# Seven block products for eight in the first product of a channel mix, on pairs of weight blocks in two passes

## The chip, the core and the metric

The kernel runs on one core of a Trainium2 chip. TensorE (PE) multiplies, VectorE (DVE) and ScalarE (ACT) work on tiles in SBUF and read PE's sums in PSUM, SyncE (SP) issues the DMAs. The metric is the device time of one execution in microseconds, as the median of three runs. Weights and inputs lie in DRAM at the start, the output is written back there.

## The reference

```python
B, H, S, D = 4, 8, 576, 64                     # tokens: 4 x 576 = 2304, columns C = 8 x 64 = 512
x = attention(q, k, v)                          # windowed and dilated heads, softmax
xk, xr = mixes of x and the token before it
v = relu(xk @ w_k) ** 2 @ w_v                   # 512 -> 1024 -> 512
x = sigmoid(xr @ w_r) * v
u = x + (relu(x^T @ w_tok1) @ w_tok2)^T         # token stage: 576 -> 256 -> 576
h2 = relu(u @ w_ch1) @ w_ch2                    # channel stage: 512 -> 1536 -> 512
out = u + h2
```

All arrays are fp32. w_ch1 is called w_c1 in the kernel, w_ch2 w_c2. The change concerns the channel stage, which computes `h2` and `out` for 2304 tokens.

## The kernel before

Stages follow one another: attention, the mix with `w_k`, `w_v` and `w_r`, the token stage, the channel stage. In the trace, the token stage's tiles begin at about 343 us and the channel stage has PE alone from about 409 us.

A matrix product in fp32 is made of parts. Each operand is split into a high half (fp32r, made by a copy) and a low half (what is left, made by a subtraction), and `mm3` (L441) issues three matmuls: high x high, high x low, low x high. A matmul has a stationary operand of 128 x 128 and a moving one of up to 512 columns. Thus one product with 512 rows in depth takes 4 x 3 matmuls for 128 rows of output.

Weights are read as pairs of 32-bit words. `weight` (L472) makes fp32 of them: a DMA into a raw tile, an ACT activation (Prelu), a DVE `tensor_scalar`, a DVE `scalar_tensor_tensor` on 16-bit halves; then the split, a copy (on ACT or DVE) and a subtraction (DVE).

The channel stage lies transposed: rows are columns of the model, columns are tokens. `u` (L822) is held in the slots `wv`, four batches of 576 tokens. It runs over chunks of 512 tokens, four full ones and a last one of 256 (L962 to L976). In each chunk:

- `prep_u` (L932) splits the four 128-row tiles of `u` into halves.
- `middle(c, m)` (L938), for 12 blocks m of 128 hidden columns, multiplies block m of `w_c1` with these four tiles into one of the PSUM banks 0 to 3, and then ACT takes the relu as the high half and DVE makes the low half.
- `result(c, m)` (L949) stands two blocks later in the program. It multiplies the 128 rows m of `w_c2` with that hidden block into banks 4 to 7, one for each 128 output rows, summed over all 12 blocks. After the last, DVE adds `u`, and a DMA on SP's queue stores the tile in `outT`.

All 24 blocks of channel weights are converted up to the end of the first chunk and stay in SBUF: four of `w_c1` ahead of the token stage in program order, the others as the first chunk comes to them (`weight_1`, `weight_2`).

The program is only recorded by that code. `Plan` keeps each operation with the operations that it depends on, and where an operation may run on ACT or DVE, both forms. `order()` (L287) is a list scheduler: it sums the costs of the PE operations in program order to due times, gives every other operation the due time that its readers need, and then, engine by engine, starts the ready operation that is due first, by a cost for each form and a delay for each pair of engines. What comes out is a fixed order for each engine's queue. `emit` issues everything from one line, so every row of the trace has that line (L399), and groups are told apart by tile names: `xt`, `x`, `wk`, `wr`, `wv`, `at`, `z`, `raw`, `unit` are slots of SBUF, `bank` is PSUM. Slots are used by several stages in turn: in the channel stage `wv` holds `u`, `xt` and `wk` hold `w_c1`, `x` (x2) and `at` hold `w_c2`, `z`, `y`, `wr` and part of `xt` hold split tokens and hidden blocks.

Of the kernel before, what the change touches and what calls it, by code (L numbers as in the profile page):

```python
# [61 lines left out]
    wk=[2048] * 4, wr=[1024] * 4, wv=[4 * S] * 4, z=[1536] * 6, y=[512],  # L62
# [85 lines left out]
class Plan:  # L148
# [35 lines left out]
    @staticmethod  # L184
    def _cells(a):
# [10 lines left out]
    def either(self, *options):  # L196
# [3 lines left out]
        local = [(k, a) for k, a in kw.items() if hasattr(a, "space") and "DRAM" not in str(a.space)]  # L200
# [212 lines left out]
def tile_model(nc, banks, units, cst, mu, w_k, w_v, w_r, w_t1, w_t2, w_c1, w_c2, outT):  # L413
# [27 lines left out]
    def mm3(out, lh, ll, rh, rl, first, last):  # L441

        nc.tensor.matmul(out=out, lhsT=lh, rhs=rh, start=first, stop=False)
        nc.tensor.matmul(out=out, lhsT=lh, rhs=rl, start=False, stop=False)
        nc.tensor.matmul(out=out, lhsT=ll, rhs=rh, start=False, stop=last)
# [31 lines left out]
    wv2 = [pair(("wv", m, 0), (2, C)) for m in range(4)]  # L477
# [9 lines left out]
    def weight(srcs, hi, lo, raw_ring, tmp_ring, zero=None):  # L487

        shape = tuple(hi.shape[1:])
        n = int(np.prod(shape))
# [12 lines left out]
        t = tmp_ring.tile(n)  # L510
# [7 lines left out]
        if len(shape) == 2:  # L518
            t = t.split(*shape)
        split(t, hi, lo)  # L520
# [21 lines left out]
    unit_r = ring(cut("wv", range(4), UQ + UK), ("z", 4, 0))  # L542
    v_r = ring(cut("wr", range(4), UV), ("z", 4, UQ + UK))
# [261 lines left out]
    for k in range(2):  # L805
# [6 lines left out]
    c1 = [  # L812
        tuple(at(xt512[2 * n + i], (4, 128), F32R) for i in range(2))
        for n in range(4)
    ]
    c1 += [pair(p, (4, 128)) for p in cut("wk", range(4), 1024)]
    c2 = [pair(p, (C,)) for p in cut("x2", (5, 6, 0, 1, 2, 3, 4), 1024)] + [pair(p, (C,)) for p in cut("at", (0,), 1024)]
    raw_c, tmp_c = ring([("wr", k, 0) for k in range(3)]), ring(cut("z", (5,), 512))
    hid_r = ring(z512[:8])
    x2h_r, x2l_r = ring(z512[9::2]), ring(z512[10::2])  # L820

    def u(b, kt, cs):  # L822
        return at(("wv", b, S * kt), (S,))[:, cs]

    def weight_1(m):
        if m < 4:
            for n in range(2):
                q = slice(2 * n, 2 * n + 2)
                weight([(everything, col_block(w_c1, m)[:, q, :])], c1[m][0][:, q, :], c1[m][1][:, q, :], raw_b, tmp_b)
        else:  # L830
            weight([(everything, col_block(w_c1, m))], *c1[m], raw_c, tmp_c)

    def weight_2(m):
        weight([(everything, words(w_c2)[rows(m), :])], *c2[m], raw_c, tmp_c)
# [5 lines left out]
    for m in range(4):  # L840
        weight_1(m)
# [25 lines left out]
    def turn(t):  # L867
# [36 lines left out]
    for t in range(13, 17):  # L904
# [150 lines left out]
```

## Time and profile before

| | before |
|---|---|
| median of three runs | 708.95 us (708.1 to 709.75) |
| profiled execution | 708.25 us, its span 706.5 us |
| busy share of the span | PE 98%, PEld 85%, DVE 54%, ACT 41%, POOL 0% |
| mean granted clock of TensorE | 0.999 |
| DMA | 56.20 MB, mean 80 GB/s |

PEld is the load of the stationary operand, which overlaps PE. The span lies within the profiled execution's time, the rest is around it. A share over the whole span mixes the stages: DVE is busy 9 tenths in the slices from about 340 to 410 us and 1 to 3 tenths after that. The chain that ended last tells through which engine the end of the program was reached, step by step backward.

### The profile page before, as it was taken

How to read it: one execution, taken by the hardware profiler on the slowest of the kernel's cores; microseconds unless marked ns; L12 is line 12 of the kernel's file. 1: busy time of each engine (PE TensorE's matmuls, PEld its weight loads, DVE VectorE, ACT ScalarE, POOL GpSimd, SP SyncE). 2: the span in 40 equal slices, each digit the busy share in tenths (PEclk: the TensorE clock that was granted, in tenths of full speed). 3: DMA queues.
4: the chain of work that ended last, by engine and by line, in shares of the span. 5: the costliest groups of instructions: out<-in, count | busy, mean ns of one | idle time of the engine just before them, and what ended most of it. 6: DMA issues, size and time to landing. Idle time of an engine off the chain costs nothing.

```text
span 706.5 us, 10519 instructions
## 1 busy us (share of the span) xinstructions
PE 692.7 (98%) x4081; PEld 599.5 (85%) x4081; DVE 382.0 (54%) x879; ACT 287.8 (41%) x818; POOL 2.1 (0%) x22
## 2 busy tenths in 40 slices
PE   7889999999999999999999999999999999999997
PEld 6678888988988888888889988888888888888897
DVE  5999995794694695774999941132123112311211
ACT  5989864582463463543778621121121111111110
POOL 0000000000000000000000000000000000000000
PEclk9999999999999999999999999999999999999999
DMA  8987333142221002013444500001001000100010
GB/s 321 389 315 275 115 95 95 49 148 84 89 79 31 16 9 66 17 31 100 133 148 150 150 0 1 1 0 60 0 1 60 0 1 0 60 1 0 8 53 31
DMA packets 27234, 56.20 MB, mean 80 GB/s; under 512 B 2480, under 2 KB 10032, under 8 KB 27184
## 3 DMA queue, kind: packets, MB, share of 16 engines
q1 hardware_dynamic: 27184, 55.53, 23.7%
q8 instruction: 32, 0.52, 0.3%
q14 instruction: 18, 0.15, 0.1%
HBM read 50.80 MB, written 4.72 MB: 79 GB/s over the span
## 4 chain that ended last, share of the span: by engine, by line
PE 88%; DMA 6%; ACT 3%; DVE 2%; issue 0%; SPq 0%; DVEq 0%; ACTq 0%
PE bank L399 88%; DMA x<-w_k 2%; ACT z L399 1%; DMA wr<-units 1%; DVE z L399 1%; ACT x L399 1%; DMA wv<-units 1%; DMA raw<-w_v 1%; DMA xt<-w_c 1%; ACT at L399 0%; DVE x L399 0%; ACT xt L399 0%; SPq L399 0%; DVE xt L399 0%; ACT wv L399 0%
## 5 line engine op out<-in xcount | busy, mean ns | idle before, releaser
L399 DVE SCALAR_TENSOR_TENSOR z<-bank,z 128x512 fp32r<-128x512 f32 (+2 forms) x116 | 69.9, 606 | 243.5 <-ACT z L399 243.4
L399 PE MATMUL bank<-z,wk 128*128 128x384 f32 (+2 forms) x816 | 197.0, 356 | 0.2
L399 ACT ACTIVATE z<-bank 128x512 fp32r<-128x512 f32 (+3 forms) x120 | 63.4, 529 | 296.7 <-PE bank L399 296.3
L399 PEld LDWEIGHTS bank<-z,wk 128*128 128x128 f32 x816 | 146.9, 188 | 15.9 <-ACT z L399 0.9
L399 PE MATMUL bank<-wv,z 128*128 128x512 f32 x432 | 129.7, 403 | 0.0
L399 PE MATMUL bank<-z,x 128*128 128x512 f32 (+1 forms) x540 | 118.4, 368 | 0.0
L399 PEld LDWEIGHTS bank<-z,x 128*128 128x128 f32 x540 | 94.8, 189 | 16.8
L399 PEld LDWEIGHTS bank<-wv,z 128*128 128x128 f32 x432 | 77.9, 188 | 11.9
L399 PE MATMUL bank<-z,at 128*128 128x512 f32 (+1 forms) x276 | 67.5, 380 | 0.0
L399 PE MATMUL bank<-wr,z 128*128 128x512 f32 x228 | 63.3, 402 | 0.9 <-DVE z L399 0.9
L399 ACT ACTIVATE at<-at 128x96 f32<-128x96 f32 (+2 forms) x150 | 48.9, 328 | 22.4 <-DVE at L399 21.3
L399 PEld LDWEIGHTS bank<-z,at 128*128 128x128 f32 x276 | 48.6, 189 | 8.0
L399 DVE TENSOR_TENSOR z<-z,z 128x384 fp32r<-128x384 f32 x92 | 50.3, 553 | 3.8 <-ACT z L399 1.8
L399 PEld LDWEIGHTS bank<-wr,z 128*128 128x128 f32 x228 | 41.3, 188 | 8.4 <-DVE z L399 1.2
L399 PE MATMUL bank<-xt,wk 128*128 128x512 f32 (+2 forms) x160 | 38.0, 369 | 1.1 <-ACT at L399 1.1
L399 PE MATMUL bank<-at,z 128*128 128x288 f32 x192 | 34.7, 302 | 1.0 <-DVE wv L399 1.0
L399 DVE SCALAR_TENSOR_TENSOR z<-xt,cst,z 128x256 f32<-128x256 f32 (+3 forms) x92 | 33.7, 403 | 0.6
L399 ACT ACTIVATE x<-bank 96x512 f32<-96x512 f32 (+1 forms) x45 | 26.4, 591 | 18.5 <-PE bank L399 18.1
L399 ACT ACTIVATE z<-z 128x384 fp32r<-128x384 f32 x56 | 28.9, 524 | 8.7 <-DVE z L399 6.6
L399 PEld LDWEIGHTS bank<-at,z 128*128 128x128 f32 x192 | 29.8, 188 | 3.1 <-DVE wv L399 1.2
L399 PEld LDWEIGHTS bank<-xt,wk 128*128 128x128 f32 x160 | 27.2, 189 | 6.0 <-issue 1.3
L399 PE MATMUL bank<-z,xt 128*128 128x512 f32 (+1 forms) x120 | 31.4, 382 | 0.0
(117 smaller groups left out, 766.0 us busy)
## 6 DMA issues: line engine op xcount, KB each, us to landing
wr<-w_c SPq DMA_DIRECT2D x20, 512.0 KB, 3.9
at<-units SPq DMA_DIRECT2D x14, 416.0 KB, 3.7
unit<-units SPq DMA_DIRECT2D x13, 416.0 KB, 3.4
at<-units SPq DMA_DIRECT2D x21, 256.0 KB, 2.8
wv<-units SPq DMA_DIRECT2D x8, 416.0 KB, 6.8
x<-w_k SPq DMA_DIRECT2D x3, 1024.0 KB, 7.3
outT<-z SPq DMA_DIRECT2D x9, 256.0 KB, 2.1
wr<-units SPq DMA_DIRECT2D x8, 256.0 KB, 6.7
```

The lines of the kernel that those rows point to most:

```text
L399: call(kw["out"], kw["constant"]) if method == "memset" else call(**kw)
```

## The change

The first product of the channel stage is computed by seven block products in place of eight. Two blocks of 128 hidden columns, j and j + 6, are a pair. The pair's weights are a 2 x 2 matrix of blocks A (two halves of the 512 rows in depth by two blocks of columns), and a chunk of 512 tokens is a 2 x 2 matrix of blocks B (two halves of the depth by 256 tokens each). Four of the eight products of blocks are replaced by products of sums: S1 to S4 are sums and differences of blocks of A, T1 to T4 of B. The seven products are A11 B11, A12 B21, S1 T1, S2 T2, S3 T3, S4 B22 and A22 T4, in the form that has few additions behind them. Each has a depth of 2 x 128 and 256 columns, thus 2 x 3 matmuls of 256 columns.

- `weight_1(j)` converts two blocks of `w_c1`, forms four sums (four DVE operations of 256 columns), and splits A11 and A12 (512 columns), A22 (256) and the sums (1024). `weight_2(j)` converts the two blocks of `w_c2`. Four pairs fit in SBUF.
- There are six pairs and two passes of three pairs, each pass over all chunks. In the first pass DVE adds `u` to the sum of three pairs and SP stores the tile in DRAM (`parts`, 20 tiles); in the second the tile is loaded, added to the other three pairs' sum, and stored in `outT`. Pairs 4 and 5 are converted in the last chunk of the first pass, in the places of pairs 0 and 1.
- `prep_u(g, c)` forms T1 to T4 (four DVE subtractions of 2 x 256 columns) and splits seven operands of 2 x 256 columns. It runs for each chunk in each pass.
- `result` follows `middle` one pair later. `middle(c, j)` uses three PSUM tiles of 256 columns. Into x (bank 0 or 1) go A11 B11, S2 T2, S3 T3 and A22 T4, into y (bank 2) S1 T1 and S4 B22, into z (bank 3) A12 B21. Products that follow in a tile are added to what lies there; between two of them the tile is read by a copy (`kept`, on ACT or DVE) or an addition (`plus`, DVE). `put` makes the halves of the hidden blocks, by 256 columns.
- The last chunk, of 256 tokens, has 24 matmuls of 256 columns per pair, as before.
- `u` now lies in two tiles `whole` of 2 x 2304 columns, the slots `wv` are two instead of four, and the rings of the attention stage's units are made of other slots (`unit_r`, `v_r`).

```diff
-    wk=[2048] * 4, wr=[1024] * 4, wv=[4 * S] * 4, z=[1536] * 6, y=[512],
+    wk=[2048] * 4, wr=[1024] * 4, wv=[8 * S] * 2, z=[1536] * 6, y=[512],
...
+    @staticmethod
+    def _kept(a):
+        return "DRAM" not in str(a.space) or a.name.startswith("part")
...
+    both = at(("raw", 0, 0), (2, 4, 128))
+    sums = at(("raw", 0, 1024), (4, 2, 128))
+    LO, HI = slice(0, 2), slice(2, 4)
+    GROUP, RESIDENT = 3, 4
...
-    c2 = [pair(p, (C,)) for p in cut("x2", (5, 6, 0, 1, 2, 3, 4), 1024)] + [pair(p, (C,)) for p in cut("at", (0,), 1024)]
+    w2 = [pair(p, (C,)) for p in cut("x2", (5, 6, 0, 1, 2, 3), 1024)]
...
+    def weight_1(j):
+
+        four, two, one, _ = w1[j % RESIDENT]
+        for i in range(2):
+            single([(everything, col_block(w_c1, j + 6 * i))], at(("raw", 0, 512 * i), (512,)), raw_c)
+        a, b = both[:, 0], both[:, 1]
+        combine(sums[:, 0], b[:, LO], b[:, HI], ALU.add)
+        combine(sums[:, 1], sums[:, 0], a[:, LO], ALU.subtract)
+        combine(sums[:, 2], a[:, LO], b[:, LO], ALU.subtract)
+        combine(sums[:, 3], a[:, HI], sums[:, 1], ALU.subtract)
+        split(a, *two)
+        split(b[:, HI], *one)
+        split(sums, *four)
+
+    both_r = ring(("raw", 0, 0), ("raw", 0, 512))
+
+    def weight_2(j):
+        for i in range(2):
+            weight([(everything, words(w_c2)[rows(j + 6 * i), :])], *w2[2 * (j % RESIDENT) + i], raw_c, both_r)
...
-    for m in range(4):
-        weight_1(m)
+    for j in range(2):
+        weight_1(j)
...
-    uhl_r = [
-        ring(xt512[8:12], cut("wr", (3,), 512), z512[14], ("y", 0, 0)),
-        ring(z512[6:14]),
-    ]
-    mid_r = ring(z512[:6])
-    o_r = ring(cut("at", (2,), 512, 2), cut("z", (5,), 512))
-    mp_r = psum(0, 1, 2, 3)
+    spare = [("wk", 1, 1536), ("wk", 3, 1536), ("xt", 0, 1536)]
+    first_r = ring(xt512[8:12], ("wr", 3, 512), z512[8:15], cut("at", (2,), 512))
+    other_r = ring(z512[:15], ("y", 0, 0))
+    mid_r = ring(cut("z", (5,), 512), spare, [("at", 0, 2048), ("at", 0, 2560)])
+    t_r = ring([("unit", i, 0) for i in range(2)])
+    part_r = ring(cut("x2", (4,), 256), cut("at", (1,), 256))
+    y_r = ring(xt512[8:12])
+    xp_r, yp_r, zp_r = psum(0, 1), psum(2), psum(3)
...
-    def prep_u(c, kt):
-        h, l = (uhl_r[c % 2].tile(size_of(c), dtype=F32R) for _ in range(2))
-        for o, b, t, n in u_pieces(c):
-            split(u(b, kt, slice(t, t + n)), h[:, o:o + n], l[:, o:o + n])
-        uhl[c, kt] = (h, l)
-
-    def middle(c, m):
+    def prep_u(g, c):
+        b1, b2 = (w[:, :, CH * c:CH * c + size_of(c)] for w in whole)
+        h = 256
+        ops = {"B11": b1[:, :, :h], "B21": b2[:, :, :h]}
+        if size_of(c) == CH:
...
+        formed = {
+            "T1": lambda: (b1[:, :, h:], ops["B11"]), "T2": lambda: (ops["B22"], ops["T1"]),
+            "T3": lambda: (ops["B22"], b1[:, :, h:]), "T4": lambda: (ops["B21"], ops["T2"]),
+            "T5": lambda: (ops["B21"], ops["B11"]),
+        }
+        for name in order:
+            if ops[name] is None:
+                x, y = formed[name]()
+                ops[name] = t_r.tile(2, h)
+                combine(ops[name], x, y, ALU.subtract)
+            r = first_r if (g, c) == (0, 0) else other_r
+            hl = r.tile(2, h, dtype=F32R), r.tile(2, h, dtype=F32R)
+            split(ops[name], *hl)
+            uhl[name] = hl
...
+    def product(out, a, b, first=True, last=True, goes_on=False):
+        for k in range(2):
+            (ah, al), (bh, bl) = w1[now % RESIDENT][3][a], uhl[b]
+            mm3(out, ah[:, k], al[:, k], bh[:, k], bl[:, k], first and k == 0, last and k == 1, goes_on)
+
+    def kept(p):
+        t = part_r.tile(256)
+        copy(t, p)
+        return t
+
+    def plus(p, t):
+        out = part_r.tile(256)
+        combine(out, p, t, ALU.add)
+        return out
...
+    def put(m, half, x):
+        h, l = (v[:, half] for v in mid[m])
+        nc.scalar.activation(out=h, in_=x, func=AF.Relu)
+        nc.vector.scalar_tensor_tensor(out=l, in0=x, scalar=0.0, in1=f(h), op0=ALU.max, op1=ALU.subtract)
...
+    def middle(c, j):
+        nonlocal now
+        now = j
+        n = size_of(c)
+        for m in (j, j + 6):
+            mid[m] = tuple(mid_r.tile(n, dtype=F32R) for _ in range(2))
+        lo, hi = slice(0, 256), slice(256, 512)
...
+        x, y, z = xp_r.tile(256), yp_r.tile(256), zp_r.tile(256)
+        product(x, "A11", "B11")
+        s1 = kept(x)
+        product(y, "S1", "T1")
+        s5 = kept(y)
+        product(z, "A12", "B21")
+        put(j, lo, plus(z, s1))
+        product(x, "S2", "T2", first=False, goes_on=True)
+        s2 = kept(x)
+        product(y, "S4", "B22", first=False, goes_on=True)
+        put(j, hi, plus(y, s2))
+        product(x, "S3", "T3", first=False, goes_on=True)
+        put(j + 6, hi, plus(x, s5))
+        product(x, "A22", "T4", first=False, goes_on=True)
+        put(j + 6, lo, x)
+
+    def result(g, c, j):
+        n, start = size_of(c), CH * c
         for kt in range(4):
...
-                    nc.vector.tensor_tensor(
-                        out=y[:, o:o + n], in0=op[kt][:, o:o + n], in1=u(b, kt, slice(t, t + n)), op=ALU.add
-                    )
-                nc.sync.dma_start(out=outT[rows(kt), CH * c:CH * c + size_of(c)], in_=y)
+            if j % GROUP == 0:
+                op[kt] = bank(4 + kt, (n,))
+            for i in range(2):
+                w = w2[2 * (j % RESIDENT) + i]
+                mm3(
+                    op[kt], w[0][:, rows(kt)], w[1][:, rows(kt)], *mid[j + 6 * i],
+                    j % GROUP == 0 and i == 0, j % GROUP == GROUP - 1 and i == 1,
+                )
+            if j % GROUP == GROUP - 1:
+                y, part = y_r.tile(n), parts[4 * c + kt][:, :n]
+                if g == 0:
+                    nc.vector.tensor_tensor(out=y, in0=op[kt], in1=whole[kt // 2][:, kt % 2, start:start + n], op=ALU.add)
+                    nc.sync.dma_start(out=part, in_=y)
+                else:
+                    nc.sync.dma_start(out=y, in_=part)
+                    nc.vector.tensor_tensor(out=y, in0=op[kt], in1=y, op=ALU.add)
+                    nc.sync.dma_start(out=outT[rows(kt), start:start + n], in_=y)
 
...
+    steps = [(g, c, j) for g in range(2) for c in range(nchunk) for j in range(GROUP * g, GROUP * g + GROUP)]
+    for i in range(len(steps) + 1):
+        if i < len(steps):
+            g, c, j = steps[i]
+            if j % GROUP == 0:
+                prep_u(g, c)
+            if (g, c, j) == (0, 0, 0):
+                weight_1(2)
+                weight_1(3)
+            middle(c, j)
+        if i:
+            before = steps[i - 1]
+            if before[:2] == (0, 0):
+                weight_2(before[2])
+            result(*before)
+            if before == (0, 0, 2):
+                weight_2(3)
+            if before[:2] == (0, nchunk - 1) and before[2] < 2:
+                weight_1(before[2] + RESIDENT)
+                weight_2(before[2] + RESIDENT)
```

The matmuls of PE become 4073 instead of 3641: 576 fewer of 512 columns and 1008 more of 256. Up to the token stage the order on all engines is as before, except for the slots of the units.

PE, before, in a full chunk: a `middle` into bank 1 (the first five rows, 12 matmuls) and a `result` into banks 4 to 7, with `xt` and `z`, `wr`, `y` as weights and tokens.

```order
L399 MATMUL bank1_62<-xt1_1_3452,xt2_1_2889 128x512 x6
L399 MATMUL bank1_62<-wr3_1_490,xt2_1_2889 128x512 x3
L399 MATMUL bank1_62<-z4_1_522,xt2_1_2889 128x512
L399 MATMUL bank1_62<-y0_1_3722,xt2_1_2889 128x512
L399 MATMUL bank1_62<-z4_1_522,xt2_1_2889 128x512
L399 MATMUL bank4_65<-z1_0_470,at0_1_2579 128x512 x3
L399 MATMUL bank5_66<-z1_0_470,at0_1_2579 128x512 x3
L399 MATMUL bank6_67<-z1_0_470,at0_1_2579 128x512 x3
L399 MATMUL bank7_68<-z1_0_470,at0_1_2579 128x512 x3
```

PE, after, in a full chunk of the second pass, pair 4: bank 3 takes A12 B21, bank 0 (with `wk0`, the sums) S3 T3, bank 2 S4 B22, bank 0 (with `wk1`) A22 T4, and bank 4 the second product of pair 3. Just ahead of these rows stand S2 T2 on bank 0, then the six of S1 T1 on bank 2.

```order
L403 MATMUL bank3_66<-z0_0_399,wk1_0_599 128x256
L403 MATMUL bank0_63<-z2_0_460,wk0_0_371 128x256
L403 MATMUL bank3_66<-z0_0_399,wk1_0_599 128x256
L403 MATMUL bank0_63<-z2_0_460,wk0_0_371 128x256 x3
L403 MATMUL bank2_65<-z1_0_490,wk0_0_371 128x256 x6
L403 MATMUL bank4_67<-wk3_1_794,x22_1_3673 128x512
L403 MATMUL bank0_63<-z2_0_460,wk1_0_599 128x256
L403 MATMUL bank0_63<-z3_0_472,wk1_0_599 128x256
L403 MATMUL bank0_63<-z2_0_460,wk1_0_599 128x256 x2
L403 MATMUL bank0_63<-z3_0_472,wk1_0_599 128x256
L403 MATMUL bank0_63<-z2_0_460,wk1_0_599 128x256
L403 MATMUL bank4_67<-xt0_1_3310,x22_1_3673 128x512
```

The matmuls of one tile now stand in groups of six with 256 columns, tile x (bank 0) comes back after one group of another tile or two, and single matmuls of tiles alternate.

DVE, before, in the fourth chunk: the low halves of hidden blocks (`z` from a bank), then the split of the last chunk's tokens (`xt` from `wv`).

```order
L399 SCALAR_TENSOR_TENSOR z1_0_470<-bank3_64,z0_0_379 128x512
L399 SCALAR_TENSOR_TENSOR z1_0_470<-bank0_61,z1_0_470 128x512
L399 SCALAR_TENSOR_TENSOR z0_0_379<-bank1_62,z0_0_379 128x512
L399 SCALAR_TENSOR_TENSOR z1_0_470<-bank2_63,z0_0_379 128x512
L399 CAST xt1_1_3452<-wv3_2_3573 128x256
L399 TENSOR_TENSOR xt1_1_3452<-wv3_2_3573,xt1_1_3452 128x256
```

DVE, after, in the second pass, in pair 5 of the chunk before that of the PE rows above: the copies of bank 0 are `kept`, the operations on `unit` form T operands, those that write `y0` and `z1` from `wv` or `unit` are splits of the next chunk, and those on `x24` and `at1` are `plus`.

```order
L403 COPY at1_2_3827<-bank0_63 128x256
L403 TENSOR_TENSOR y0_1_4049<-unit0_0_364,z4_1_542 128x512
L403 TENSOR_TENSOR unit0_0_364<-wv1_2_3206,wv0_2_3201 128x512
L403 COPY x24_0_188<-bank0_63 128x256
L403 TENSOR_TENSOR z1_0_490<-wv1_2_3206,z1_0_490 128x512
L403 TENSOR_TENSOR x24_0_188<-bank3_66,at1_2_3827 128x256
L403 TENSOR_TENSOR at1_2_3827<-bank0_63,x24_0_188 128x256
L403 TENSOR_TENSOR z1_0_490<-unit1_0_373,z0_0_399 128x512
L403 TENSOR_TENSOR x24_0_188<-bank2_65,x24_0_188 128x256
L403 SCALAR_TENSOR_TENSOR z5_1_3855<-x24_0_188,z5_1_3855 128x256
```

The short operations that read banks of 256 columns stand between operations of 512 columns on the tokens of the next chunk.

DVE, before, where the token stage ends and channel weights are converted: `wr` holds raw words, `z5` a block in work, `wk1` a split weight, `z4` from `x23` split tokens, and the rows on `wv1` of 288 columns add the token stage's product to `u`.

```order
L399 SCALAR_TENSOR_TENSOR z5_0_358<-wr0_2_3066,z5_0_358 128x512
L399 TENSOR_TENSOR wv1_2_3264<-bank6_67,wv1_2_3264 128x288
L399 TENSOR_TENSOR wk1_0_579<-z5_0_358,wk1_0_579 128x512
L399 TENSOR_SCALAR z5_0_358<-z5_0_358 128x512
L399 TENSOR_TENSOR wv1_2_3264<-bank7_68,wv1_2_3264 128x288
L399 TENSOR_TENSOR z4_1_522<-x23_0_337,z4_1_522 128x512
L399 SCALAR_TENSOR_TENSOR z5_0_358<-wr1_2_3079,z5_0_358 128x512
```

DVE, after, at the token stage's beginning: `raw0` holds the pair's two blocks and its four sums, `wk0` and `wk3` the split weights; the rows from `x26` split tokens, and `x24` with a bank are from the stage before.

```order
L403 TENSOR_TENSOR wk0_0_371<-raw0_0_317,wk0_0_371 128x1024
L403 TENSOR_TENSOR z4_1_542<-x26_0_724,z4_1_542 128x512
L403 SCALAR_TENSOR_TENSOR x24_0_188<-x24_0_188,bank6_69 128x512
L403 SCALAR_TENSOR_TENSOR x24_0_188<-x24_0_188,bank7_70 128x512
L403 SCALAR_TENSOR_TENSOR raw0_0_317<-wr1_2_3070,raw0_0_317 128x512
L403 TENSOR_TENSOR wk3_1_794<-raw0_0_317,wk3_1_794 128x512
L403 TENSOR_TENSOR raw0_0_317<-raw0_0_317 128x256
L403 TENSOR_TENSOR z3_0_472<-x26_0_724,z3_0_472 128x512
L403 TENSOR_TENSOR raw0_0_317<-raw0_0_317 128x256 x3
```

Sums of 256 columns and a split of 1024 come in between; the conversion of a pair of `w_c1` is a longer chain on DVE.

## Rows read from the trace of the kernel before

**Rows 1.** The page: the span, and the chain that ended last, by engine.

```profile
span 706.5 us, 10519 instructions
...
PE 88%; DMA 6%; ACT 3%; DVE 2%; issue 0%; SPq 0%; DVEq 0%; ACTq 0%
```

**Rows 2.** Windows: stretch, us, busy of five engines, clock, DMA share, GB/s.

```profile
343.00:371.00 28.00, 27.02 (x162) 23.50 (x161) 27.15 (x59) 22.40 (x56) 0.00 (x0) 1.00 0.45 141
371.00:409.00 38.00, 38.00 (x240) 34.81 (x239) 37.96 (x83) 26.78 (x58) 0.00 (x0) 1.00 0.46 139
409.00:470.00 61.00, 61.00 (x271) 50.51 (x270) 14.35 (x28) 10.52 (x20) 0.00 (x0) 1.00 0.00 1
470.00:662.00 192.00, 192.00 (x849) 158.99 (x848) 38.85 (x75) 23.13 (x41) 0.00 (x0) 1.00 0.05 17
663.00:698.00 35.00, 35.00 (x273) 34.02 (x272) 7.33 (x19) 4.22 (x11) 0.00 (x0) 1.00 0.08 31
```

**Rows 3.** Timeline of PE, channel stage: start, duration, operation, out<-in, count.

```profile
654.48 2.88 PE L399 MATMUL bank<-z,x 128*128 128x512 f32 x12
657.20 2.88 PE L399 MATMUL bank<-z,wk 128*128 128x512 f32 x12
...
675.31 1.60 PE L399 MATMUL bank<-z,x 128*128 128x256 f32 x12
676.75 0.88 PE L399 MATMUL bank<-xt,wk 128*128 128x256 f32 x6
```

**Rows 4.** Timeline of PE: the token stage and the end.

```profile
343.02 0.60 PE L399 MATMUL bank<-cst,x 128*128 128x128 f32 x4
343.37 0.94 PE L399 MATMUL bank<-wv,z 128*128 128x512 f32 x3
...
406.48 1.76 PE L399 MATMUL bank<-at,z 128*128 128x288 f32 x12
408.08 0.40 PE L399 MATMUL bank<-xt,xt 128*128 128x512 f32 x1
...
698.35 4.48 PE L399 MATMUL bank<-z,at 128*128 128x256 f32 x36
```

**Rows 5.** Timeline of DVE and PE, token stage; in brackets: idle before, its releaser.

```profile
342.70 0.67 DVE L399 SCALAR_TENSOR_TENSOR x<-x,bank 128x512 f32<-128x512 f32 x1
...
365.99 0.46 DVE L399 TENSOR_TENSOR wv<-bank,wv 128x288 f32<-128x288 f32 x1
...
366.50 0.67 PE L399 MATMUL bank<-at,z 128*128 128x288 f32 x3 [0.98 <-DVE wv L399]
...
408.28 0.46 DVE L399 TENSOR_TENSOR wv<-bank,wv 128x288 f32<-128x288 f32 x1
```

**Rows 6.** Timeline of PE and ACT at a tile's end in the channel stage.

```profile
420.33 0.39 PE L399 MATMUL bank<-z,xt 128*128 128x512 f32 x1
...
420.76 0.60 ACT L399 ACTIVATE z<-bank 128x512 fp32r<-128x512 f32 x1 [4.84 <-PE bank L399]
```

**Rows 7.** Timeline of DVE, operations one behind another in the token stage.

```profile
363.27 0.42 DVE L399 TENSOR_SCALAR z<-z 128x512 uint32<-128x512 uint32 x1
363.60 0.45 DVE L399 TENSOR_TENSOR wv<-bank,wv 128x288 f32<-128x288 f32 x1
363.97 0.75 DVE L399 SCALAR_TENSOR_TENSOR z<-wr,z 128x512 uint16<-128x512 uint32 x1
364.60 0.69 DVE L399 TENSOR_TENSOR z<-x,z 128x512 fp32r<-128x512 f32 x1
365.19 0.70 DVE L399 SCALAR_TENSOR_TENSOR z<-bank,z 128x512 fp32r<-128x512 f32 x1
```

**Rows 8.** Groups of one shape: count | busy us, mean ns | idle before, releaser.

```profile
L399 ACT ACTIVATE wv<-bank 128x256 f32<-128x256 f32 x32 | 10.3, 389 | 4.0 <-PE bank L399 4.0
...
L399 DVE SCALAR_TENSOR_TENSOR z<-bank,z 128x256 fp32r<-128x256 f32 x12 | 5.1, 425 | 30.2 <-ACT z L399 30.2
```

**Rows 9.** DMA issues of the output: count, KB each, median us to landing.

```profile
outT<-z SPq DMA_DIRECT2D x9, 256.0 KB, 2.1
```

More of the change, by code (lines that the diff above doesn't have):

```diff
@@ L439, in psum, with mm3 @@
         return Ring(bank, numbers)
[L441 to L445, printed above, removed]
+    def mm3(out, lh, ll, rh, rl, first, last, goes_on=False):
+        more = dict(skip_group_check=True) if goes_on else {}
+        nc.tensor.matmul(out=out, lhsT=lh, rhs=rh, start=first, stop=False, **more)
+        nc.tensor.matmul(out=out, lhsT=lh, rhs=rl, start=False, stop=False, **more)
+        nc.tensor.matmul(out=out, lhsT=ll, rhs=rh, start=False, stop=last, **more)
     def copy(out, in_):
@@ L476, in tile_model @@
     wr = [pair(("wr", k, 0), (C,)) for k in range(4)]
[L477 removed]
+    wv2 = [pair(("wv", m // 2, 4 * S * (m % 2)), (2, C)) for m in range(4)]
     wv = [tuple(w[:, i, :] for w in ws) for ws in wv2 for i in range(2)]
@@ L517, in weight @@
         )
-        if len(shape) == 2:
-            t = t.split(*shape)
-        split(t, hi, lo)
+    def weight(srcs, hi, lo, raw_ring, tmp_ring, zero=None):
+        shape = tuple(hi.shape[1:])
+        t = tmp_ring.tile(int(np.prod(shape)))
+        single(srcs, t, raw_ring, zero)
+        split(t.split(*shape) if len(shape) == 2 else t, hi, lo)
     everything = slice(0, 128)
@@ new lines, in tile_model, with operands @@
+    sums = at(("raw", 0, 1024), (4, 2, 128))
+    LO, HI = slice(0, 2), slice(2, 4)
+    GROUP, RESIDENT = 3, 4
+    def operands(four, two, one):
+        four, two, one = pair(four, (4, 2, 128)), pair(two, (4, 128)), pair(one, (2, 128))
+        named = {f"S{i + 1}": tuple(v[:, i] for v in four) for i in range(4)}
+        named.update({f"A1{i + 1}": tuple(v[:, 2 * i:2 * i + 2] for v in two) for i in range(2)}, A22=one)
+        return four, two, one, named
+    w1 = [
+        operands(("wk", 0, 0), ("wk", 1, 0), ("wk", 1, 1024)),
+        operands(("wk", 2, 0), ("wk", 3, 0), ("wk", 3, 1024)),
+        operands(("xt", 2, 0), ("xt", 0, 0), ("xt", 0, 1024)),
+        operands(("at", 0, 0), ("wr", 2, 0), ("wr", 3, 0)),
+    ]
@@ L833, in weight_2 @@
-    def weight_2(m):
-        weight([(everything, words(w_c2)[rows(m), :])], *c2[m], raw_c, tmp_c)
+        return whole[kt // 2][:, kt % 2, S * b:S * b + S][:, cs]
     def tiles_of(b):
@@ new lines, in tile_model @@
+    now = 0
+    def middle(c, j):
[5 more added lines that the diff above has]
+        lo, hi = slice(0, 256), slice(256, 512)
+        if n < CH:
+            x, y = xp_r.tile(256), yp_r.tile(256)
+            product(x, "A11", "B11", last=False)
+            product(x, "A12", "B21", first=False)
+            put(j, lo, x)
+            product(y, "S1", "B11", last=False)
+            product(y, "A22", "T5", first=False)
+            put(j + 6, lo, y)
+            return
+        x, y, z = xp_r.tile(256), yp_r.tile(256), zp_r.tile(256)
[13 more added lines that the diff above has]
+        put(j + 6, lo, x)
@@ L1045 @@
     with tile.TileContext(nc) as tc:
-        with tc.tile_pool(name="memory", bufs=1) as pool, tc.tile_pool(name="sums", bufs=1, space=PSUM) as sums:
+        with tc.tile_pool(name="memory", bufs=1) as pool, tc.tile_pool(name="sums", bufs=1, space=PSUM) as sums, tc.tile_pool(
+            name="parts", bufs=1, space=bass.MemoryType.DRAM
+        ) as dram:
             banks = [sums.tile([128, 512], F32, name=f"bank{i}", tag=f"bank{i}") for i in range(8)]
+            parts = [dram.tile([128, CH], F32, name=f"part{i}", tag=f"part{i}") for i in range(4 * -(-NT // CH))]
             plan = Plan(nc)
-            tile_model(plan, banks, *aps, out)
+            tile_model(plan, banks, parts, *aps, out)
             with tc.manual_schedule():
```

78 lines of the change are left out of this document (17 added, 61 removed).

## The prediction

> **What bounds the kernel now.** The page comes first [rows 1]. The span is 706.5 us, and the chain that ended last lies on PE for 88% of it. Then the work by stage, in stretches that I chose from the tile names [rows 2]: in the channel stage, from about 409 us to the end, PE is busy in every microsecond at full granted clock (1.00, the level of 2.4 GHz), while DVE works 14.35 of 61 us and then 38.85 of 192. What shortens the channel stage is PE work alone. The stretch ahead of it is different: from 343 to 409 us DVE works 65.1 of 66 us, since it prepares tokens and converts all channel weights there, and PE loses 0.98 us to it visibly [rows 2, 5]. So two questions decide: how much PE work goes, and whether DVE, which gets more to do, becomes the bound around 343 to 440 us.
>
> **PE work, the first term.** Matmuls overlap, so their cost is the step from start to start, not the duration. With 512 columns, 12 of one tile begin at 654.48 and the next tile's at 657.20: 2.72/12 = 0.2267 us each. With 256 columns, 12 begin at 675.31 and the next at 676.75: 1.44/12 = 0.120 us each [rows 3]. Both rows are of the same two products, each matmul with new weights. Halving the columns saves less than half: 0.0067 us more than half is paid each time.
> Before, a pair of weight blocks takes 2 x 4 x 3 = 24 matmuls of 512 columns in a full chunk, 24 x 0.2267 = 5.44 us. Now it takes seven products of 2 x 3 matmuls of 256, 42 x 0.120 = 5.04 us. That is 0.40 us per pair and chunk; with 6 pairs and 4 full chunks 24 x 0.40 = 9.6 us. The last chunk of 256 tokens has 24 matmuls of 256 columns per pair before and after: nothing. The second product keeps its matmuls, 24 of 512 or 256 per pair and chunk. So a step of one pair is 5.04 + 5.44 = 10.48 us of PE, where it was 10.88.
> The Trainium skill (TensorE: Matmul & The Clock Gate, "Back-to-back issue gap") gives for a sustained stream of weight load and matmul about 81 ns at 128 columns and 131 ns at 512; a straight line between, my estimate, is 98 ns at 256. By that the change would cost 42 x 98 - 24 x 131 = 0.97 us per step, 23 us in all. This trace does not agree: its 226.7 and 120.0 ns are far above both.
>
> **The turns of the PSUM tiles, the second term.** Before, `middle` has four banks and never returns to one soon. Now one x tile of 256 columns takes four products in turn, and between them a copy or an addition must have read it; the order shows the two narrow places. From S2 x T2 to S3 x T3 (both on x) PE has six matmuls of the y tile and three of z between; from S3 x T3 to A22 x T4 it has six of y and one of the second product, which begins the next group 0.12 + 6 x 0.12 + 0.227 = 1.07 us after the last matmul's start.
> What must happen in that time is read from the steady state [rows 6]: the last matmul of a group starts at 420.33 and ACT begins at 420.76, 0.43 later; with 256 columns that is 0.11 us less, so 0.32, since the matmul itself takes 1.60 - 11 x 0.120 = 0.28 instead of 0.39 [rows 3, 6]. A read of 256 columns takes 0.39 on ACT or 0.42 on DVE [rows 8]. From DVE's end to the waiting PE it is 0.05 (366.45 to 366.50) [rows 5]. The sum is 0.76 to 0.79, against 1.07 and, at the other place, 1.20. So both are covered by 0.28 to 0.4 us, if the reading engine is free. It is not always: each chunk brings DVE 11 subtractions and split halves of 512 columns, 0.60 us each [rows 7], among the step's own short ones. In a full chunk I count 41 DVE instructions: 15 of 512 columns x 0.60 and 26 of 256 x 0.34 [rows 7, 8], 17.8 us of 31.4. A step whose copy stands behind one of these in the queue waits up to 0.60 - 0.28 = 0.32 us. The bounds are nothing, and 24 steps x 2 places x 0.32 = 15 us. The order puts the long ones mostly behind the short ones, so I take 1 us, near the lower bound.
>
> **The transition, the third term.** From the first `x<-x,bank` at 342.70 to the end of the first chunk's first pass I count 194 DVE instructions in the new order: 66 with two inputs of 512 columns x 0.60 = 39.6; 15 of the kind uint16 x 0.63 = 9.5; 32 token additions of 288 columns x 0.37 = 11.8; 55 of 256 columns x 0.34 = 18.7 (0.425 long, less the 0.09 by which neighbours overlap); 4 of 1024 columns, an estimate, x 1.15 = 4.6; 22 shorter ones x 0.35 = 7.7 [rows 5, 7, 8]. In all some 92 us. PE has in the same stretch, from 343.02, 6 + 120 matmuls of 512 columns, 192 of 288 at 0.133 (12 in 1.60 us), 72 transposes at 0.0875 (4 in 0.35) and three steps: 28.6 + 25.5 + 6.3 + 31.4 = 91.8 us; the order puts 55 matmuls of the next chunk ahead of the last of these, 6.6 more, 98.4 in all [rows 3, 4]. DVE is thus 93% full for 98 us, where before it was 99% full for 66.
> Before, PE's own work up to the last token product is 28.6 + 25.5 + 6.3 + 1.4 of the channel stage = 61.8 us, and it ended at 408.08, after 65.1 us [rows 4]; DVE worked without a gap from 342.70 to the last token addition, 408.28 + 0.46 [rows 5]. So about 3 us were lost to DVE. What moves: pairs 0 to 3 of the first weights and pairs 0 to 3 of the second are converted here instead of all twelve blocks of each, but each pair brings four sums and 1792 instead of 1024 columns to split, and seven instead of four operands are made from the tokens. Up to the last token addition the new order has 62.3 us of DVE work, so there the loss can shrink to nothing; in the first chunk it may come back. Between 3 us less and 6 us more (a tenth of the 66 us) I take no difference, since the fill is much as before.
>
> **What else moves.** Ahead of 343 us the order of PE, SP and nearly all of DVE and ACT is as before, apart from the unit slots: nothing. Twenty stores of 256 KB and as many loads come to the queue of SP. Each such store lands in 2.1 us [rows 9], a pass has one group of four every 31 us, and the first use of a loaded part is a whole chunk after its place is free; hidden. Without that cover four such transfers in a row would be 4 x 2.1 = 8.4 us per chunk. Pairs 4 and 5 are converted at the pass boundary, into operands that the last chunk has just left; some 13 us of DVE in 48 us. The end is the same chain, four additions and four stores behind the last matmul (698.35 + 4.48 = 702.83 to 706.5) [rows 1, 4].
>
> **The sum.** -9.6 (products) + 1 (turns) + 0 (transition) = -8.6 us. The profiled execution is 708.25 us, its span 706.5 and 1.75 around it; that makes 699.65. The median of the three runs is 708.95, 0.7 above the profiled one, so I forecast 700.3.
>
> **The rivals.**
> (a) DVE becomes the bound in the transition. For it: 93% full for longer, and a chain of sums and splits that must end ahead of each new pair. Against it: PE lost only 3 us to a fuller DVE before, and the order begins the second pair's products early where the first's operands are late. It would cost 3 to 6 us more: 703 to 706.
> (b) The turns are not covered, and the kernel gets slower. Place: the copies and additions on the x tile, each step, on DVE and ACT. The point from which it decides is 9.6/24 = 0.40 us of PE waiting per step. One 0.60 us instruction ahead at both narrow places gives 0.64 per step, 15.4 us: 708.95 - 9.6 + 15.4 = 714.8. Against it is the slack of 0.28 and more, and that DVE is idle 40% of a chunk.
> (c) 256-column matmuls that alternate with 512-column ones don't keep their 0.120 us, because the weight load for each matmul no longer fits beneath the one ahead. The break-even is 5.44/42 = 0.1295 us; at 0.140 the change costs 24 x 42 x 0.020 - 9.6 = 10.6 us, 719.5. For it: PEld is busy 34.02 of 35 us in the last chunk [rows 2], hardly below full. Against it: there each matmul does have new weights, and the step is 0.120 without exception. The rule of the Trainium skill above (TensorE: Matmul & The Clock Gate, "Back-to-back issue gap") would be its far end, 708.95 + 23 = 732; no row bears that out, and of (c)'s chance 0.01 is for it.
> (d) The transition loses less than before, and the turns cost nothing: 708.95 - 9.6 - 2 = 697.3 or so.
>
> **How the numbers follow.** The forecast 0.60 (698.5 to 702.5), (a) 0.19, (b) 0.06, (c) 0.03, (d) 0.12. About 0.2% (1.4 us) is what a measurement of this kernel can tell from no change. Faster by more than that: the forecast, (d), and (a) almost whole, 0.90. Within it: the upper end of (a) and the mild part of (b), 0.03. Slower: the rest of (b), and (c), 0.07. The range for 8 in 10 leaves out the lowest of (d), the upper part of (a), (b) and (c): 697.6 to 705.
>
> **What would show it.** In the profile after, 432 more matmuls; the steps 0.120 and 0.227 in the channel stage, and a full chunk of one pass in 31.4 us. A wait of PE on DVE or ACT with 256 columns in the channel stage, above 0.1 us per step in the mean, is (b); the PE busy time in the windows from 343 to 440 us shows (a), with idle ended by DVE; a step above 0.125 where kinds alternate is (c). The last matmul should start its group some 8.6 us earlier than now, and 3.6 us remain behind it. I am wrong in the main if the channel stage's PE sum is right and PE is idle in it all the same.

## The result and the profile after

| kernel | median of runs | ratio to before, 95% interval |
|---|---|---|
| before, same group of runs | 709.35 us (708.1 to 710.0) | |
| changed | 703.35 us (702.46 to 704.08) | 0.9917 (0.9898 to 0.9936) |
| changed, second group of runs | 701.69 us (before: 708.29) | 0.9910 (0.9897 to 0.9924) |

The change gains 6.0 to 6.6 us, where 8.65 were forecast (708.95 to 700.3). Both medians lie in the range of 697.6 to 705; the first lies above the narrower stretch of the forecast itself (698.5 to 702.5), the second in it. The page of the changed kernel: span, and the chain by engine, beside [rows 1].

```profile
span 702.3 us, 11861 instructions
...
PE 87%; DVE 5%; DMA 4%; ACT 2%; issue 1%; SPq 0%; DVEq 0%; ACTq 0%
```

The windows of the changed kernel, columns and stretches as [rows 2]:

```profile
343.00:371.00 28.00, 27.15 (x156) 23.46 (x157) 28.00 (x56) 20.36 (x47) 0.00 (x0) 1.00 0.31 96
371.00:409.00 38.00, 36.79 (x235) 33.38 (x234) 32.55 (x69) 16.01 (x35) 0.00 (x0) 1.00 0.29 92
409.00:470.00 61.00, 60.83 (x394) 55.35 (x393) 50.77 (x108) 27.52 (x62) 0.00 (x0) 1.00 0.17 56
470.00:662.00 192.00, 192.00 (x1241) 174.97 (x1240) 125.55 (x268) 64.94 (x147) 0.00 (x0) 1.00 0.21 69
663.00:698.00 35.00, 35.00 (x239) 32.47 (x238) 11.14 (x24) 5.08 (x12) 0.00 (x0) 1.00 0.14 46
```

The channel stage stays with PE, though DVE now works 125.55 of 192 us. From 371 to 409 us PE is idle for 1.2 us and DVE for 5.5.

This execution also lost time early: from 17 to 40 us its clock was granted at 0.85 in the mean, before at 1.00, and by the starts of equal matmuls it went from 0.6 us ahead of the kernel before (at 18 us) to 1.2 us behind it (at 290 us). The second group's profile has 1.00 there and a span of 699.9 us; I compare with that one, 6.6 us below 706.5.

Where the time went is counted from the starts of all matmuls: from each step the plain step of its width is taken (226.7 ns for 512 columns, 120.0 for 256, 133.5 for 288, 87.5 for the transposes of 128), and what is left, the excess, is summed, from 291 to 429 us (the transition) and from there to the last matmul (the channel stage). Matmuls of 384 columns, of the stage before, are left out.

| kernel | transition, us | channel stage, us | changes of width in it |
|---|---|---|---|
| before | 4.2 | 0.0 | 5 |
| changed, first group | 7.0 | 2.0 | 354 |
| changed, second group | 5.9 | 2.1 | 352 |
| passes alone | 5.3 | 0.0 | 9 |
| pair 3 later | 6.7 | 1.7 | 354 |
| grouped | 7.3 | 1.2 | 125 |
| spread | 6.1 | 1.7 | 747 |
| four banks | 4.3 | 1.8 | 351 |
| four banks, grouped (two groups of runs) | 4.2, 4.3 | 1.2, 1.2 | 128, 127 |
| the same, pair 1 later | 5.0 | 1.2 | 127 |
| four banks, one group per result | 3.6 | 1.75 | 55 |
| the same, load first | 3.0 | 1.7 | 54 |

So -9.6 (products) + 2.1 (channel stage) + 1.7 (transition) - 0.56 (the end) = -6.4; between the two spans, 706.5 and 699.9, -6.6 were measured.

### The profile page after: what moved, and what is told of

Its sections match the earlier page's. It is cut to its first block, busy times and chain, and to the rows that moved or that the text cites. A ratio compares the mean times of both kernels' runs of the same rounds, so it can differ in the third digit from the quotient of the medians.

```text
span 702.3 us, 11861 instructions
## 1 busy us (share of the span) xinstructions
PE 687.2 (98%) x4513; PEld 612.5 (87%) x4513; DVE 500.1 (71%) x1125; ACT 332.1 (47%) x930; POOL 2.1 (0%) x22
## 4 chain that ended last, share of the span: by engine, by line
PE 87%; DVE 5%; DMA 4%; ACT 2%; issue 1%; SPq 0%; DVEq 0%; ACTq 0%
PE bank L403 87%; DVE z L403 2%; ACT z L403 1%; DMA x<-w_k 1%; DMA wr<-units 1%; DVE x L403 1%; DMA wv<-units 1%; DMA xt<-w_t 1%; DVE at L403 1%; DVE xt L403 0%; DVE raw L403 0%; DVE wv L403 0%; ACT x L403 0%; DVE unit L403 0%; ACT at L403 0%
## 5 line engine op out<-in xcount | busy, mean ns | idle before, releaser
L403 PE MATMUL bank<-z,wk 128*128 128x256 f32 (+1 forms) x1276 | 242.8, 311 | 0.3 <-DVE z L403 0.2
L403 PEld LDWEIGHTS bank<-z,wk 128*128 128x128 f32 x1276 | 201.9, 189 | 11.8 <-DVE z L403 0.8
L403 PE MATMUL bank<-z,x 128*128 128x512 f32 (+1 forms) x300 | 80.8, 371 | 0.0
L403 ACT ACTIVATE z<-bank 128x384 f32<-128x384 f32 (+3 forms) x78 | 36.6, 473 | 74.7 <-PE bank L403 73.9
L403 PE MATMUL bank<-wk,x 128*128 128x512 f32 (+1 forms) x180 | 66.3, 371 | 0.0
L403 ACT ACTIVATE at<-at 128x96 f32<-128x96 f32 (+3 forms) x155 | 51.1, 332 | 21.8 <-DVE at L403 20.6
L403 ACT ACTIVATE x<-bank 96x512 f32<-96x512 f32 (+2 forms) x68 | 35.1, 519 | 51.5 <-PE bank L403 50.4
L403 PEld LDWEIGHTS bank<-z,x 128*128 128x128 f32 x300 | 52.3, 189 | 7.0
L403 PE MATMUL bank<-at,x 128*128 128x512 f32 (+1 forms) x180 | 53.7, 372 | 0.0
L403 PE MATMUL bank<-z,at 128*128 128x256 f32 (+1 forms) x196 | 46.0, 342 | 0.0
```

The costliest lines, as they stand in the source:

```text
L403: call(kw["out"], kw["constant"]) if method == "memset" else call(**kw)
```

## The experiments

**The changed kernel again.** 

> The changed kernel once more, as the measure for the others of this group. All theories: some 703.4 us, 0.992 of the kernel before.


701.69 us, 0.9910: the measure for the next three.

**Pair 3 later.**

```diff
+            if (g, c, j) == (0, 1, 1):
                 weight_1(3)
...
-            if before == (0, 0, 2):
+            if before == (0, 1, 1):
                 weight_2(3)
```

> The conversion of pair 3, which the first pass does not use, moves from the first chunk to the second. It is some 8.5 us of DVE work (by the rows' steps: 5.4 for the four sums, shifts and splits of w_c1, 3.1 for w_c2). Theory A (the 2.8 us that PE waits more than before from 340 to 440 us are lost because DVE is full there): the waits at 412 to 426 us, some 2 us, go; the one of 1.27 us at 353 us stays, since pair 3 comes after it. 701 to 702 us, about 1.5 to 2 below the changed kernel. Rival B (those waits are the length of chains from a PSUM tile to the next matmul, not the amount of DVE work): the same waits stay, change within 0.5 us. PE's steps in the channel stage don't change by either.


701.96 us, 0.9913 (0.9899 to 0.9926): no gain. The two waits at 400 us, 0.51 and 0.60 us in the changed kernel, are here as they were (0.51 and 0.59), and so is the one of 0.19 at 413 us. As a test of theory A this is weaker than meant: other work of DVE moved up into the room, so that from 343 to 425 us DVE was busy for 78.9 us where it had been for 76.4, and less only from 425 to 440 us (10.6 in place of 13.2). What a less busy DVE would do there isn't shown by it. The windows of the changed kernel (second group) and of this one, columns as [rows 2]:

```profile
409.00:425.00 16.00, 15.81 (x109) 14.53 (x109) 15.90 (x35) 10.28 (x23) 0.00 (x0) 1.00 0.11 34
```
```profile
409.00:425.00 16.00, 15.81 (x111) 14.64 (x110) 15.93 (x34) 9.96 (x23) 0.00 (x0) 1.00 0.00 1
```

Against theory A speaks what DVE did just ahead of the two waits. The timeline of the changed kernel (second group), DVE and PE:

```profile
395.69 0.82 DVE L403 TENSOR_TENSOR wv<-bank,wv 128x288 f32<-128x288 f32 x2 [1.11 <-PE bank L403]
...
397.92 1.75 PE L403 MATMUL bank<-at,z 128*128 128x288 f32 x12
398.12 0.30 DVE L403 CAST wr<-raw 128x256 fp32r<-128x256 f32 x1 [1.60 <-PE bank L403]
398.32 1.28 DVE L403 SCALAR_TENSOR_TENSOR z<-bank,z 128x512 fp32r<-128x512 f32 x2
...
399.57 0.82 DVE L403 TENSOR_TENSOR wv<-bank,wv 128x288 f32<-128x288 f32 x2
...
400.18 1.81 PE L403 MATMUL bank<-at,z 128*128 128x288 f32 x12 [0.51 <-DVE wv L403]
...
402.07 0.82 DVE L403 TENSOR_TENSOR wv<-bank,wv 128x288 f32<-128x288 f32 x2
...
402.58 1.84 PE L403 MATMUL bank<-at,z 128*128 128x288 f32 x12 [0.60 <-DVE wv L403]
```

DVE is idle for 1.11 and 1.60 us just ahead. PE fills both banks of the token product, and their last matmuls start 0.13 us apart, at 399.24 and 399.37; DVE begins to add at 399.57, 0.33 after the first of them, and PE begins again. Before, a matmul of the first chunk (`xt,xt`, 408.08) stood between such groups [rows 4]; now PE has nothing else.

**Grouped, and spread.** Grouped: `nc.burst` around each product and each result tile, so that its six matmuls stay together. Spread: in the scheduler's due times the matmuls of a result are put evenly among those of the products.

```diff
+        start = len(nc.ops)
         for k in range(2):
...
+        nc.burst(start, 0.0)
```
```diff
+            keys = [((k + 0.5) / len(p), i) for k, i in enumerate(p)] + [((k + 0.5) / len(q), i) for k, i in enumerate(q)]
+            for place, (_, i) in zip(sorted(p + q), sorted(keys)):
+                sequence[place] = i
```

> The order keeps the six matmuls of a product, and the six of a result tile, together: matmuls of 256 and of 512 columns follow each other 131 times instead of 373 in the last 1860. Theory C (each such change of length costs some 5 ns, which makes the 2 us that the channel stage lost against steps of 226.7 and 120.0 ns): 131/373 of 2 us are left, the PE steps sum up to 1.3 us less, some 702. Rival D (the longer steps of 512 columns, 230 ns in the mean, come from DVE and ACT working beside PE): they stay, 703.4. Where whole products wait for their last operand, up to 1 us can be lost in the transition by either.

> The opposite: the order spreads the matmuls of a result among those of the products, 787 changes of length instead of 373. Theory C: 414 more at 5 ns, 2.2 us more, some 705.6, with mean steps of 512 columns above 230 ns. Rival D: steps as in the changed kernel, 703.4.


702.47 us, 0.9915 (0.9902 to 0.9929), and 702.16 us, 0.9920 (0.9906 to 0.9934). Neither tells in the time; the steps do. The timeline of PE in the grouped kernel:

```profile
473.80 0.88 PE L403 MATMUL bank<-z,wk 128*128 128x256 f32 x6
474.51 0.40 PE L403 MATMUL bank<-wk,x 128*128 128x512 f32 x1
474.74 0.40 PE L403 MATMUL bank<-xt,x 128*128 128x512 f32 x1
474.98 0.39 PE L403 MATMUL bank<-wk,x 128*128 128x512 f32 x1
475.20 0.85 PE L403 MATMUL bank<-at,x 128*128 128x512 f32 x3
475.89 0.28 PE L403 MATMUL bank<-z,wk 128*128 128x256 f32 x1
...
478.00 0.39 PE L403 MATMUL bank<-wk,x 128*128 128x512 f32 x1
478.22 0.39 PE L403 MATMUL bank<-xt,x 128*128 128x512 f32 x1
478.45 0.39 PE L403 MATMUL bank<-wk,x 128*128 128x512 f32 x1
478.68 0.84 PE L403 MATMUL bank<-at,x 128*128 128x512 f32 x3
479.36 3.76 PE L403 MATMUL bank<-z,wk 128*128 128x256 f32 x30
```

Behind a run of 256 columns six matmuls of 512 take 475.89 - 474.51 = 1.38 us, 0.23 each; the six from 478.00, which follow others of 512, take 1.36, 0.2267 each. In nanoseconds, over all 63 runs of 512 in this stage of the grouped kernel: the first five steps have a mean of 233.6, 235.7, 228.3, 232.4 and 230.5, 27 more than five plain ones, from the sixth on 227, and the first of 256 behind them takes 113, 7 less than plain. That is 0.0195 us per run, 63 x 0.0195 = 1.23, what the table has.

Rival D falls: the first step of a run is 233.6 in the mean whether DVE works through most of it (41 runs) or hardly at all (16), and the same goes for ACT (19 and 41 runs); from the sixth on the steps are plain either way. Theory C is right in its place and wrong in its rule: the price goes by runs and by their length, not by changes, so that 747 changes in the spread kernel, with short runs, cost no more than 352. The five steps are those of the grouped kernel, where at least six matmuls of 256 columns stand ahead of each run. In the changed kernel single matmuls of both widths stand ahead of the runs of eight or nine, and there the sixth to the ninth step still have a mean of 230. What the rule is in such a mixture, and why the price is paid at all, stays open.

Grouping lost in the transition what it gained; it has a wait of 1.17 us near 343 us (below).

**Four banks; four banks and grouped from the second chunk on.**

```diff
-                hp = up_r.tile(HALF)
+                hp = (up_r if b < 2 else wide_r).tile(HALF)
```

`wide_r` takes the banks 6, 7, 4 and 5 in turn.

> The token stage's last product, for batches 2 and 3, takes its PSUM tiles from four banks (4 to 7) instead of two. Theory B (the waits of 0.51 and 0.60 us at 400 and 402 us are the chain from a tile of 288 columns over DVE's addition to the next product that needs the bank, while the channel stage's first operands are not there yet): both waits go, 1.1 us less than the changed kernel, some 700.6 us. Theory A, what is left of it (DVE has no time there): the waits stay within 0.3 us; against it DVE was idle for 1.1 and 1.6 us just ahead of them.

> The four banks, and from the second chunk on the matmuls of a product or a result tile kept together. If the cost of a change of length is paid in the first five matmuls of 512 columns of a run, some 0.02 us for a whole run, with 60 runs instead of 176: 0.9 us less in the channel stage, beside the 1.1 of the banks, some 699.7. If a matmul of 512 columns is longer for another reason, 700.6.


700.44 us, 0.9884 (0.9868 to 0.9900), and 699.90 us, 0.9876 (0.9857 to 0.9896). Theory B holds: the two waits are gone, and PE runs through the token product with four banks, as its timeline shows:

```profile
395.77 7.50 PE L403 MATMUL bank<-at,z 128*128 128x288 f32 x54
```

In the matmuls of that product for batches 2 and 3 the excess is 0.35 us, where it was 2.1. The grouping takes another 0.6 us off in the channel stage, where 0.9 was expected.

**Passes alone.** The same passes and stores, plain first product:

```diff
+        for m, w in zip((j, j + 6), w1[j % RESIDENT]):
+            x = xp_r.tile(n)
+            for kt in range(4):
+                mm3(x, w[0][:, kt, :], w[1][:, kt, :], *uhl[kt], kt == 0, kt == 3)
+            put(m, slice(0, n), x)
```

> Pairs, two passes, partial sums in DRAM and u in two tiles, but the first product with its eight block products as plain 24 matmuls of 512 columns, no sums, four token tiles split per chunk and pass. If the seven products bring the whole gain: PE's matmuls are those of the kernel before, and the time is that of before, 708.3, down to 706.5 where the transition has less to convert. If the passes are what makes it faster: about 702. If the passes cost something that the products had to make good: above 709.


707.71 us, 0.9989 (0.9980 to 0.9999). In the median the passes cost nothing and give 0.8 us; the rest of the gain is the seven products'. At the end they give 0.56 (below).

**Six products.**

```diff
-        product(x, "A22", "T4", first=False, goes_on=True)
```

> The changed kernel without the product A22 T4 in full chunks (the hidden block of it lacks that part). 24 pairs and chunks times 6 matmuls of 256 columns. If the stage is bound by PE at 0.120 us each: 17.3 us less, some 684.4. If DVE, now at 60 to 70% there, or the turns of the x tile come to bind: 687 or more.


This kernel leaves the product A22 T4 out of its sums, so it tells what a product costs and nothing else. 683.93 us, 0.9654 (0.9633 to 0.9675): 17.8 us below the 701.69 of the changed kernel in its second group, and no wait of PE is listed from 429 to 690 us. The stage is bound by PE, near the plain step.

**One group per result, four banks and grouped again, and pair 1 later.** The 24 matmuls of a result in one group; and `weight_1(1)` behind the token stage with pair 3 in the second chunk.

```diff
             result(*before)
+            if before[:2] != (0, 0):
+                nc.burst_of([i for i in range(at_first, len(nc.ops)) if "tensor" in nc.ops[i]])
```
```diff
-    for j in range(2):
-        weight_1(j)
+    weight_1(0)
...
+                weight_1(1)
                 weight_1(2)
```

> As the kernel with four banks and groups, but all 24 matmuls of a result in one group: 77 changes of length in place of 149. By the price found there (a whole run of 512 columns behind a run of 256 costs 0.0195 us in all), some 34 runs instead of 64 from 440 us on: 0.6 us less, 699.3. If the turns of the x tile are uncovered by it (S3 T3 to A22 T4 may stand with nothing between): up to 24 x 0.5 = 12 us more.

> The kernel with four banks and groups once more, as the measure for the others of this group: some 699.9 us.

> As the kernel with four banks and groups, but pair 1 is converted behind the token stage in program order, and pair 3 in the second chunk. Theory A (the wait near 341 to 353 us, 0 to 1.3 us by the execution, comes from DVE, which has sums and splits of pair 1 in its queue ahead of the token splits): that wait goes, 0.5 to 1 us less, some 699.2. Rival B: the wait is a chain from the stage before and stays, and pair 1 comes late for the second step of the first chunk: 700 to 702.


699.10 us, 0.9865 (0.9848 to 0.9883); 699.38, 0.9863 (0.9845 to 0.9880); 699.63, 0.9871 (0.9855 to 0.9887). One group saves runs: the 28 that are left should cost 28 x 0.0195 = 0.55, but the excess is 1.75. The turns of the x tile are now uncovered, as the timeline of PE shows, where 31 matmuls take 478.83 - 475.03 = 3.80 us in place of 3.72. In 17 places a matmul that waits for a copy on ACT (`kept`), which ended 0.07 us before its start, has a step of 0.20 in place of 0.12, 1.41 us in all; no wait is listed for them.

```profile
475.03 3.96 PE L411 MATMUL bank<-z,wk 128*128 128x256 f32 x31
...
478.83 1.09 PE L411 MATMUL bank<-z,x 128*128 128x512 f32 x4
```

With pair 1 later the wait near 342 us did not go; it shows what it is. The timeline of that kernel, ACT, DVE and PE:

```profile
341.80 0.37 ACT L403 ACTIVATE xt<-xt 128x192 f32<-128x192 f32 x1 [2.12 <-DMA xt<-w_t]
...
342.20 0.26 DVE L403 TENSOR_SCALAR xt<-xt 128x192 uint32<-128x192 uint32 x1 [1.88 <-ACT xt L403]
...
343.52 1.21 PE L403 MATMUL bank<-wv,z 128*128 128x512 f32 x4 [1.56 <-DVE z L403]
```

The last piece of `w_tok2` lands late, DVE stands behind its conversion in a fixed order, and PE behind DVE. The piece now stands behind a load of pair 1 of `w_c1` on SP's queue, as the timelines of that queue show, before and after (second group):

```profile
335.59 0.33 SPq L399 DMA_DIRECT2D xt<-w_t  x1
336.70 0.33 SPq L399 DMA_DIRECT2D wr<-w_c  x1
```
```profile
334.03 0.37 SPq L403 DMA_DIRECT2D wr<-w_c  x1
335.26 0.34 SPq L403 DMA_DIRECT2D xt<-w_t  x1
```

In the changed kernel, first group, it is the same chain, 1.66 on the DMA and 1.11 us on PE; in the second ACT waited 0.48 and PE not at all.

**Load first.** Pair 1's load of 512 KB goes behind that piece on SP's queue.

```diff
+            if j == 1:
+                nc.deps[load].add(t2_load)
```

> As the kernel with one group per result, but the load of pair 1's first block of w_c1 waits for the issue of the last piece of w_tok2, so that piece stands ahead of it on SP's queue. In the runs so far the conversion of that piece waits on its DMA, 0.3 to 2.1 us, and PE loses 0 to 1.7 us near 342 us. If the load of 512 KB ahead of it is the cause: ACT's wait on that DMA is under 0.5 us and PE has no wait there; the median is up to 0.6 us below that of the kernel it starts from, 698.5 to 699.1. If it isn't, the wait shows as often as before, 699.1 or more.


698.86 us, 0.9865 (0.9848 to 0.9881). ACT no longer waits on that DMA (the piece's activation begins at 339.53 with no wait shown) and PE has none there, in the one profile; the order of other instructions moved a little too. From issue to landing the piece took 2.45 us here and 2.35 in the kernel before, and 3.7 to 5.9 us in the twelve other profiles, which all have the load of 512 KB just ahead of it: it is the place in the queue that makes it land late. Why the time differs so much between those twelve stays open. In time the kernel is level with the one it started from, since that one's profile had no wait there either; what the late load costs in the median isn't separable here. Its ratio can't be told from those of the last three kernels, and its interval lies below that of the changed kernel: 0.9881 at most against 0.9897 at least.

## Why the prediction was right, and which sizes were off

The mechanism held: less PE work in a stage that PE bounds. That the gain fell no more than 2 to 2.7 us short owes something to luck: two costs that the sum had at nothing, 2.1 and 1.7 us, were in part balanced by two terms that came out better, by some 0.9 and 0.56 us.

- **Products, -9.6: right in mechanism.** 432 more matmuls, PE without a gap, six products 17.8 us less where 17.3 was reckoned. What the step missed is 2.1 us: "the step is 0.120 without exception" held for 256 columns (mean 119.4 ns in the changed kernel from 429 us on), but [rows 3] showed each width in long runs only, and it is the matmuls of 512 columns that pay (mean 231.9 ns, and 235.9 directly behind one of 256). Rival (c) was right about alternation as a cause and wrong about who pays and how much, 2.1 of the 9.6 us it needed. The rule of the Trainium skill (TensorE: Matmul & The Clock Gate, "Back-to-back issue gap") gives 131 ns at 512 columns, and the prediction's estimate from it 98 at 256; no run here comes near, at 226.7 and 120.0 where the steps are plain.
- **Turns, taken at +1: 0.1.** This term was mis-sized, upward; the chain is 0.05 us longer than reckoned. At 480.74 DVE adds on tile x, 0.37 after the start of its last matmul (480.37, from the list of all matmuls), where 0.32 was taken; of 175 groups of 256 columns from 429 us on, 69 are first read at 0.32, as reckoned, and 66 at 0.36 to 0.40. The addition ends at 481.15, and A22 T4 begins 0.29 later, at 481.44; with 0.05 for the handing over, 0.24 are to spare (forecast 0.28 to 0.4). One turn wasn't covered: at 615.00 a group begins 0.05 behind the addition that it waits for, and its first step is 0.22, 0.1 more than plain. No other step of 256 columns from 429 to 690 us is above 0.14. The timeline of the changed kernel, second group:

```profile
480.74 0.41 DVE L403 TENSOR_TENSOR at<-bank,x 128x256 f32<-128x256 f32 x1
...
481.21 0.40 PE L403 MATMUL bank<-z,x 128*128 128x512 f32 x1
481.44 0.76 PE L403 MATMUL bank<-z,wk 128*128 128x256 f32 x5
```

  From 430 to 690 us no wait of PE is listed. The long DVE instructions ahead of a copy, of which the bound of 15 us was made, don't fall on the narrow places.
- **Transition, taken at 0: +1.7 us, in the first profile +2.8.** DVE is as full as reckoned (28.00 + 32.55 and 29.94 from 409 to 440 us, 93% of 97 us), but the sum of its work is not what the longest waits came from: DVE was idle just ahead of the two at 400 us, and two more banks took them away. The step failed in looking at DVE's work in sum. Of the 1.7 us, the token products of batches 2 and 3 lose 1.8, where two PSUM banks have nothing to fill the time (waits of 1.1 us and longer steps around them), that of batch 1 0.4, and the first chunk behind them 0.7. Against this the wait of 0.98 us of before [rows 5] is gone, as the prediction said that it might; the product of batch 0, where it stood, gains 1.2. A late DMA adds 0 to 1.6 us by the execution. That one comes from a term that the prediction put at nothing: it took the order ahead of 343 us as unchanged, on SP too, and a load of pair 1 had moved ahead of the last piece of `w_tok2` there. So (a) had its place about right and its cause wrong.
- **The end, taken as before: -0.56.** From the start of the last matmul to the span's end it is 3.35 us, was 3.91, and 3.35 with the passes alone too. A result is now two hidden blocks, so a bank gets six last matmuls, 0.72 us, not three. The timeline of the end, DVE and SP's queue, before and after (second group):

```profile
702.15 1.14 DVE L399 TENSOR_TENSOR z<-bank,wv 128x256 f32<-128x256 f32 x3
...
702.67 1.37 SPq L399 DMA_DIRECT2D outT<-z  x3
```
```profile
695.19 2.49 SPq L403 DMA_DIRECT2D outT<-xt  x4
...
696.89 0.42 DVE L403 TENSOR_TENSOR xt<-bank,xt 128x256 f32<-128x256 f32 x1 [0.29 <-PE bank L403]
```

  Before, three issues in a row ended 704.04 - 703.29 = 0.75 us behind the last addition, now 697.68 - 697.31 = 0.37.

## What to carry to other kernels

A step read from a long run of one width is not the step of a mixed order: look for a stretch where the kinds alternate, or put a price on each return. An engine that is 93% full beside the critical one need not be what that one waits for; read what it did just ahead of each wait, and whether another bank or another piece of work could fill it. A wait that differed between executions of one kernel came from a DMA here, whose place in the queue the change had moved; compare the order of each queue, not only of the engines.

## What was not expected of the hardware

- In the grouped kernel, behind six or more matmuls of 256 columns, the first five of 512 take 233.6, 235.7, 228.3, 232.4 and 230.5 ns in place of 226.7; the first of 256 behind them takes 113 in place of 120.
- In two executions of the changed kernel the conversion of one load of 192 KB began at 339.61 and at 342.12 us; 1.3 of the difference is the later issue of the load in the second (336.60 against 335.26), 1.2 the load itself (5.4 us to landing against 4.3). With no load of 512 KB just ahead of it on the queue, it took 2.35 and 2.45 us.
